# Last keys' scores at an earlier tick in a bank of their own, and part of the sums and statistics of attention on ScalarE, in a Conformer block

## The chip, the cores and the metric

The kernel runs on one core of a Trainium2 chip. The metric is device time in microseconds of one execution. TensorE does the matrix products (PE, with its weight loads as PEld), VectorE (DVE), ScalarE (ACT) and GpSimd (POOL) the rest, and nearly all transfers are started by SyncE's queue (SP).

## The reference

```python
B, T, D, K = (2, 4000, 512, 3);  F = 4 * D
h = _layernorm(x);  h = _silu(h @ w_ff1_a) @ w_ff1_b;  x1 = x + 0.5 * h
h = _layernorm(x1);  q = h @ w_q;  k = h @ w_k;  v = h @ w_v
p = _softmax(jnp.einsum('btd,bsd->bts', q, k) * scale)
x2 = x1 + jnp.einsum('bts,bsd->btd', p, v) @ w_o
h = _layernorm(x2) @ w_pw1
h = h[..., :D] * _sigmoid(h[..., D:])
dc = <three taps along t of h, weights dw>
dc = <normalized per channel over all of B and T>
x3 = x2 + _silu(dc) @ w_pw2
h = _layernorm(x3);  h = _silu(h @ w_ff2_a) @ w_ff2_b;  x4 = x3 + 0.5 * h
return _layernorm(x4)
```

All arrays are bf16.

## The kernel before

**Stages.** The 8000 tokens are cut into 16 chunks (`NCK`), eight for each batch (`TCB`): seven of 512 tokens and a short one of 416. Feed-forward 1 runs over all chunks (0 to 395 us of the profile), then attention over all chunks of queries (395 to 1395), the tail of the convolution (1395 to 1435), and feed-forward 2 (1435 to the end). The layer normalization, projection and first pointwise product of the convolution for chunk `g - 1` run beside the attention of chunk `g`.

**Attention.** A chunk `g` is a loop over 32 ticks `kt`, one for each tile of 128 keys; the last tile has 32 keys. Products are done with seven multiplications in place of eight (on halves). Scores come in quads of four key tiles (`score_quad`, four steps, one for each tick): seven partial products into PSUM banks s0, s1 and s2, with ScalarE copying one bank into another and into SBUF and VectorE adding in between; a later matmul adds onto what VectorE or ScalarE left in the bank. ScalarE's exps write the probabilities. `pair_sums` makes the sums that the products with the values need, and in steps 4 and 5 the row sums of the softmax in an fp32 accumulator `acc`. The products with the values go to banks s3 and y0 to y3.

**The last 32 keys** are handled by `tail_scores`: 16 small matmuls (4 on each of four parts of the array), an exp, a store of the result to DRAM and four loads that spread it over the partitions. It stands at tick 21.

**Beside it** for chunk `g - 1`: at tick 2 `split_sums` splits the row sums into two bf16 parts, two transposing transfers turn them (`sums_by_query`), and VectorE reduces them and takes the reciprocal; at ticks 9 and 13 `project` multiplies two token tiles each by the folded value and output weights, and `residual` adds them, scaled by the reciprocal, to the stream `XT`. Then `ln_job` takes the statistics on VectorE (`bn_stats`, `bn_aggr`), the power -1/2 on GpSimd, the shift on VectorE, the normalization on ScalarE, and a transposing transfer. At ticks 24 and 28, and 3 and 5 of the next chunk, `pw1` uses the result.

**The planner.** The program is written down in this order by ticks, but not issued in it. `Plan` records every operation with the buffers it reads and writes and a duration by a formula (an activation: 170 + 0.83 ns for each element, 200 more where the scale is a per-partition operand), and draws up one order for each engine. TensorE may take matmuls from up to 8 us ahead of the oldest one left. For each other engine the operation with the earliest deadline `late` goes first; `late` is worked back from what waits for it:

```python
n.late = min([s.late - self.lag(n, s) - (self.SPARE if n.size else 0) for s in n.succs] + [pe[min(n.at, len(pe) - 1)].late + 40000])
```

The program also holds a second branch (`any_score`), for inputs with large scores; it does not run here.

In the profile nearly every instruction has line 93, so tiles are named by their memory: `sums` (probabilities and their sums), `keys`, `work` (queries, normalized tokens, row sums, small statistics), `xt` (the residual stream and the streamed key and value sums), `wff` (weights, convolution buffers, `pq` and `ptail` of the last keys), `s` and `y` (the PSUM banks).

Of the kernel before, what the change touches and what calls it, by code (L numbers as in the profile page):

```python
# [15 lines left out]
TILE = 128  # L16
# [93 lines left out]
class Plan:  # L110
# [161 lines left out]
    def once(self):  # L272

        pe, T = self.pe, self.T
        for n in reversed(self.nodes):
            if n.e != "PE":
                n.late = min([s.late - self.lag(n, s) - (self.SPARE if n.size else 0) for s in n.succs] + [pe[min(n.at, len(pe) - 1)].late + 40000])
        free = {e: 0.0 for e in self.AFTER}
# [272 lines left out]
class Conformer:  # L551
# [35 lines left out]
    def memory(self):  # L587
# [503 lines left out]
    def ln_norm(self, c, sl, ti, out, b_out, eng, src=None):  # L1091
# [7 lines left out]
        else:  # L1099
            self.act(out, x, AF.Identity, [b_x, self.b_sh[sl][ti], self.b_rs[sl][ti]], [b_out],  # L1100
                     bias=self.sh[sl][:, ti:ti + 1], scale=self.rs[sl][:, ti:ti + 1])

    def ln_job(self, c, kind, eng="DVE", plan=(1, 1, 2, 2, 3, 4, 5, 5, 6, 6), slot=None, pe=None):

# [120 lines left out]

    def residual(self, ps, b_ps, g, scalar, b_scalar=(), rows=slice(0, TILE)):

        self.S.op("DVE", lambda e: e.scalar_tensor_tensor(
            out=self.XT[g][rows], in0=ps[rows], scalar=scalar, in1=self.XT[g][rows], op0=ALU.mult, op1=ALU.add),
            reads=[b_ps, self.bx[g]] + list(b_scalar), writes=[self.bx[g]])  # L1230

# [524 lines left out]
    def pair_sums(self, g, j, step):  # L1756
# [20 lines left out]
        if step == 6:  # L1777
            S.op("DVE", lambda e: e.tensor_tensor(out=acc[:, 0], in0=acc[:, 0], in1=acc[:, 1], op=ALU.add),
                 reads=[self.b_acc[s]], writes=[self.b_acc[s]])
            return  # L1780
        sig = [ft[:, 0:2, at + k, 0:hw] for k in range(n)]
        if j == 0:
            S.op("DVE", lambda e: e.tensor_copy(acc, sig[0]), reads=b_f[0:2], writes=[self.b_acc[s]])
        elif j == GROUPS - 1:
            S.op("DVE", lambda e: e.tensor_tensor(out=acc, in0=acc, in1=sig[step - 4], op=ALU.add),
                 reads=b_f[0:2] + [self.b_acc[s]], writes=[self.b_acc[s]])
        else:
            two = self.P30[:, 0:W].rearrange("p (h k) -> p h k", h=2)
            out, x, y, rd, b_out = ((two, sig[0], sig[1], b_f[0:2], self.b_P30), (acc, acc, two, [self.b_P30, self.b_acc[s]], self.b_acc[s]))[step - 4]
            S.op("DVE", lambda e: e.tensor_tensor(out=out, in0=x, in1=y, op=ALU.add), reads=rd, writes=[b_out])  # L1790

# [153 lines left out]
    def k_stream(self, g, q):  # L1945
        n, b = (QUADS * g + q) % 2, g // TCB
        self.load(self.KF[n].rearrange("p m u j k -> p (m u j k)"), self.kfd[b][q], self.b_KF[n], reads=[self.b_kfd[b][q]])

# [54 lines left out]

    ASIDE = {3: (5, 7), 4: (5, 7), 5: (5, 7), 6: (5, 7), 16: (0,), 20: (0,), 21: (1,)}
# [148 lines left out]
    def keys_swap(self, g, kt):  # L2153
# [30 lines left out]
    def tail_scores(self, g):  # L2184
# [69 lines left out]
    def sums_by_query(self, s, n=6):  # L2254
# [5 lines left out]
        def reduce():  # L2260
            S.op("DVE", lambda e: e.tensor_reduce(
                self.sq[s], self.sT[0:TILE].rearrange("p h c k -> p c h k"), AX.XY, ALU.add),
                reads=self.b_sT, writes=[self.b_sq[s]])
            S.op("DVE", lambda e: e.reciprocal(self.rl[s], self.sq[s]), reads=[self.b_sq[s]], writes=[self.b_rl[s]])

# [7 lines left out]

    def project(self, g, ti):
        s, r = g % 2, tile_rows(g, ti)
# [7 lines left out]
        self.residual(ps, b_ps, tile_at(g, ti), self.rl[s][r, ti:ti + 1], [self.b_rl[s]], r)  # L2283

# [67 lines left out]
    def pw1(self, t, cb):  # L2352
# [9 lines left out]
        for out, x in moves:  # L2362
            for cc in range(DC):
                self.mm(out, self.Wp1[:, cc, cb * 128:(cb + 1) * 128], x[:, cc], cc == 0, cc == DC - 1,
                        [self.b_Wp1] + self.b_lnT[1 if t == NCK - 1 else 0], b_ps)
        return ps, b_ps
# [207 lines left out]
    def program(self, any_score):  # L2574
# [111 lines left out]
        def att_hook(g, kt):  # L2686
# [285 lines left out]
```

## Time and profile before

| | |
|---|---|
| time, median of 3 runs | 1879.53 us (1877.93 to 1880.09) |
| the profiled execution's own time | 1879.47 us |
| its span in the profile | 1875.6 us |
| granted TensorE clock, mean | 0.998 |
| busy: PE, PEld, DVE, ACT, POOL | 1857.5, 1445.4, 1548.0, 1278.0, 124.2 us |
| feed-forward 1, attention, tail of the convolution, feed-forward 2 | 395, 1000, 40, 441 us |
| one quiet chunk of attention | 62.93 us |

A row of the timeline gives the start of a group of equal instructions, the time to the end of the last, the engine, what it writes and reads, the shapes, the count, and in brackets how long the engine stood idle before it and which engine's result ended that. A row of grouped instructions gives the summed busy time, the mean of one in ns, and the idle time before them.

### The profile page before, as it was taken

How to read it: one execution, taken by the hardware profiler on the slowest of the kernel's cores; microseconds unless marked ns; L12 is line 12 of the kernel's file. 1: busy time of each engine (PE TensorE's matmuls, PEld its weight loads, DVE VectorE, ACT ScalarE, POOL GpSimd, SP SyncE). 2: the span in 40 equal slices, each digit the busy share in tenths (PEclk: the TensorE clock that was granted, in tenths of full speed). 3: DMA queues.
4: the chain of work that ended last, by engine and by line, in shares of the span. 5: the costliest groups of instructions: out<-in, count | busy, mean ns of one | idle time of the engine just before them, and what ended most of it. 6: DMA issues, size and time to landing. Idle time of an engine off the chain costs nothing.

```text
span 1875.6 us, 38994 instructions
## 1 busy us (share of the span) xinstructions
PE 1857.5 (99%) x15384; PEld 1445.4 (77%) x15384; DVE 1548.0 (83%) x3293; ACT 1278.0 (68%) x2190; POOL 124.2 (7%) x241
## 2 busy tenths in 40 slices
PE   9999999999999999999999999999999999999998
PEld 5888888866777777777677777777764888888886
DVE  7789989868778888877878788778878889889885
ACT  5777777754556666666557666666657787777774
POOL 1000000000000000000000001000011000000010
PEclk9999999999999999999999999999999999999999
DMA  7333344197545555448954444444365222221211
GB/s 197 86 89 91 80 112 107 53 275 208 172 142 159 155 171 160 117 130 175 254 123 133 134 119 114 126 138 122 107 205 158 66 69 69 72 54 48 63 33 56
DMA packets 325013, 231.51 MB, mean 123 GB/s; under 512 B 204179, under 2 KB 295638, under 8 KB 324566
## 3 DMA queue, kind: packets, MB, share of 16 engines
q1 hardware_dynamic: 324294, 228.68, 44.2%
q8 instruction: 123, 2.02, 0.4%
q14 instruction: 68, 0.56, 0.1%
q10 hardware_dynamic: 528, 0.26, 0.0%
HBM read 128.44 MB, written 55.79 MB: 98 GB/s over the span
## 4 chain that ended last, share of the span: by engine, by line
PE 97%; DVE 1%; ACT 1%; DMA 0%; issue 0%; SPq 0%; DVEq 0%; ACTq 0%
PE s L93 49%; PE y L93 49%; DVE work L93 1%; ACT work L93 0%; DVE wff L93 0%; DMA xt<-in_x_dram 0%; ACT sums L93 0%; DVE xt L93 0%; DVE s L93 0%; ACT xt L93 0%; ACT s L93 0%; DVE sums L93 0%; DVE keys L93 0%; ACT keys L93 0%; SPq L93 0%
## 5 line engine op out<-in xcount | busy, mean ns | idle before, releaser
L93 ACT ACTIVATE sums<-s 128x512 bf16<-128x512 f32 (+2 forms) x494 | 289.1, 587 | 234.3 <-PE s L93 232.8
L93 ACT ACTIVATE keys<-s 128x512 bf16<-128x512 f32 (+2 forms) x284 | 165.2, 587 | 141.4 <-PE s L93 115.8
L93 DVE TENSOR_TENSOR sums<-sums 128x512 bf16<-128x512 bf16 (+3 forms) x528 | 201.8, 399 | 63.5 <-ACT sums L93 53.1
L93 PE MATMUL y<-work,keys 128*128 128x256 bf16 x1920 | 244.8, 273 | 0.0
L93 PE MATMUL s<-work,keys 128*128 128x256 bf16 (+5 forms) x1456 | 225.1, 292 | 0.8 <-ACT sums L93 0.6
L93 PE MATMUL y<-wff,keys 128*128 128x256 bf16 (+3 forms) x1592 | 209.2, 276 | 0.1
L93 DVE BATCH_NORM_STATS2 work<-xt 128x6 f32<-128x512 bf16 x311 | 205.6, 683 | 3.9 <-DMA xt<-in_x_dram 3.3
L93 PEld LDWEIGHTS y<-work,keys 128*128 128x128 bf16 x1920 | 187.9, 98 | 25.1
L93 PE MATMUL y<-sums,keys 128*128 128x256 bf16 (+1 forms) x1440 | 204.8, 270 | 0.0
L93 PE MATMUL s<-sums 128*128 128x256 bf16 x1296 | 194.5, 273 | 0.0
L93 DVE TENSOR_TENSOR keys<-keys 128x1024 bf16<-128x1024 bf16 (+2 forms) x262 | 170.2, 663 | 26.2 <-ACT keys L93 20.8
L93 PE MATMUL y<-work,wff 128*128 128x256 bf16 (+2 forms) x1116 | 184.0, 292 | 0.0
L93 PEld LDWEIGHTS y<-wff,keys 128*128 128x128 bf16 (+1 forms) x1592 | 151.2, 98 | 32.4 <-issue 3.3
L93 ACT ACTIVATE work<-xt,work 128x512 bf16<-128x512 bf16 x208 | 160.1, 805 | 10.9 <-DVE work L93 9.1
L93 POOL TENSOR_TENSOR work<-work 128x4 f32<-128x4 f32 (+3 forms) x92 | 88.3, 963 | 1108.3 <-DVE work L93 1108.3
L93 PEld LDWEIGHTS y<-sums,keys 128*128 128x128 bf16 x1440 | 139.1, 98 | 22.7 <-issue 0.2
L93 PEld LDWEIGHTS s<-work,keys 128*128 128x128 bf16 (+1 forms) x1456 | 119.3, 97 | 48.2 <-issue 4.7
L93 PEld LDWEIGHTS s<-sums 128*128 128x128 bf16 x1296 | 126.7, 98 | 20.0
L93 PE MATMUL s<-work,wff 128*128 128x512 bf16 (+5 forms) x668 | 140.5, 345 | 1.4 <-ACT work L93 1.1
L93 PE MATMUL y<-sums,xt 128*128 128x256 bf16 (+1 forms) x960 | 141.2, 270 | 0.3 <-DVE sums L93 0.3
L93 PE MATMUL s<-work 128*128 128x512 bf16 (+4 forms) x565 | 137.5, 373 | 2.4 <-DVE work L93 1.7
L93 PEld LDWEIGHTS y<-work,wff 128*128 128x128 bf16 x1116 | 108.2, 98 | 29.7
(140 smaller groups left out, 3195.8 us busy)
## 6 DMA issues: line engine op xcount, KB each, us to landing
xt<-kfd SPq DMA_DIRECT2D x98, 384.0 KB, 3.2
xt<-v12d SPq DMA_DIRECT2D x105, 256.0 KB, 3.0
xd<-xt SPq DMA_DIRECT2D x28, 512.0 KB, 3.0
xt<-xd SPq DMA_DIRECT2D x28, 512.0 KB, 3.8
out_dram<-xt SPq DMA_DIRECT2D x14, 512.0 KB, 2.9
xt<-in_x_dram SPq DMA_DIRECT2D x13, 512.0 KB, 4.1
dcvd<-wff SPq DMA_DIRECT2D x48, 128.0 KB, 2.7
keys<-dcvd SPq DMA_DIRECT2D x12, 512.0 KB, 4.0
```

The source lines that it names most:

```text
L93: return getattr(eng, self.name)(*self.args, **self.kw)
```

## The change

1. `tail_scores` stands at tick 9 in all chunks but the first (there at 21, as before), ahead of the projection, and always takes bank s1.
2. `touch`: where a short chunk's query product leaves the last 96 columns of bank s1 unwritten, one more matmul of 96 columns is done onto them.
3. In `pw1` the second part of a short chunk's product no longer starts with a replacing matmul.
4. Row sums (`pair_sums`): the first group's sums are no longer copied into `acc`; they are added with the first pair's sum. The last group's two sums are first added to each other in bf16, in a new buffer `last7`.
5. Head sums (`sums_by_query`): in place of VectorE's reduce, four ScalarE copies with an accumulator output.
6. Statistics of the normalization ahead of the convolution: `residual` gives the row sum of each token as accumulator output; GpSimd makes the negative mean of it; ScalarE's Square with that as bias gives the sum of squares as accumulator output; GpSimd does the rest (`ln_middle`, `ln_spread`, `ln_rest`, `ln_beside` in place of `ln_job`).
7. The load of the last key tile of the second batch stands 18 ticks earlier.
8. The planner's deadline `late` is at least the time of the operation's own place on TensorE less 8 us.

```diff
-                n.late = min([s.late - ... for s in n.succs] + [pe[min(n.at, len(pe) - 1)].late + 40000])
+                n.late = max(pe[min(n.at, len(pe) - 1)].late - 8000, min([s.late - ... for s in n.succs] + [pe[min(n.at, len(pe) - 1)].late + 40000]))
...
+        self.last7, self.b_last7 = C.view(oLT + 4096, CHUNK), C.buf("last7", oLT + 4096, 2 * CHUNK)
-        self.b_sq = [Buf("sq") for _ in range(2)]
+        self.b_sqs = [[Buf("sq") for _ in range(TPC)] for _ in range(2)]
...
+    def touch(self, ps, b_ps, W):
+        if W < CHUNK and b_ps is self.bank(1)[1]:
+            x = self.hT[0][:, 0, 0, :]
+            self.mm(ps[:, W:CHUNK], x, x[:, 0:CHUNK - W], False, True, [self.b_hT[0][0]], b_ps, skip_group_check=True)
...
+    def ln_middle(self, sl, two):
+        self.S.op("POOL", lambda e: e.tensor_scalar(self.mv[sl][:, two, 0], self.st[sl][:, two, 0], -1.0 / D, None, ALU.mult),
+                  reads=self.b_st[sl][two], writes=self.b_mv[sl][two])
+
+    def ln_spread(self, c, sl, ti):
+        x, b_x = self.tokens(c, ti)
+        self.act(self.ltm[ti][0:TILE, :], x, AF.Square, [b_x, self.b_mv[sl][ti]], [self.b_ltm[ti], self.b_st[sl][ti]],
+                 bias=self.mv[sl][:, ti, 0:1], accum_out=self.st[sl][:, ti, 1:2])
+
+    def ln_rest(self, sl):
+        S = self.S
+        S.op("POOL", lambda e: e.tensor_scalar(self.mv[sl][:, :, 1], self.st[sl][:, :, 1], 1.0 / D, EPS, ALU.mult, ALU.add), ...)
+        S.op("POOL", lambda e: e.tensor_tensor(out=self.rs[sl], in0=self.mv[sl][:, :, 1], in1=self.neghalf[0:TILE], op=ALU.pow), ...)
+        S.op("POOL", lambda e: e.tensor_tensor(out=self.sh[sl], in0=self.mv[sl][:, :, 0], in1=self.rs[sl], op=ALU.mult), ...)
+
+    def ln_beside(self, c, sl, plan):
+        spread, rest, norm = plan[0:4], plan[4], plan[5:9]
+        def tile(ti):
+            self.ln_norm(c, sl, ti, self.ltm[ti][0:TILE, :], self.b_ltm[ti], "ACT")
+            self.transpose(self.lnT[0][:, ti], self.ltm[ti], [self.b_ltm[ti]], [self.b_lnT[0][ti]])
+        for ti in range(TPC):
+            self.after(spread[ti], lambda ti=ti: self.ln_spread(c, sl, ti))
+        self.after(rest, lambda: self.ln_rest(sl))
+        for ti in range(TPC):
+            self.after(norm[ti], lambda ti=ti: tile(ti))
...
     # residual: accum_out=total where a total is given
...
     # q_group, and pw1 where t < NCK - 1
+        self.touch(ps, b_ps, W)
...
     # pair_sums
+        if j == 0:
+            return
         sig = [ft[:, 0:2, at + k, 0:hw] for k in range(n)]
-        if j == 0:
-            S.op("DVE", lambda e: e.tensor_copy(acc, sig[0]), reads=b_f[0:2], writes=[self.b_acc[s]])
-        elif j == GROUPS - 1:
-            S.op("DVE", lambda e: e.tensor_tensor(out=acc, in0=acc, in1=sig[step - 4], op=ALU.add), ...)
+        t, b_t = (self.P30, self.b_P30) if j < GROUPS - 1 else (self.last7, self.b_last7)
+        two = t[:, 0:W].rearrange("p (h k) -> p h k", h=2)
+        if step == 4:
+            out, x, y, rd, wr = two, sig[0], sig[1], b_f[0:2], [b_t]
+        elif j == 1:
+            _, _, f0, b_0 = self.p_home(g, 0)
+            out, x, y, rd, wr = acc, two, f0[:, 0:2, 1, 0:hw], [b_t] + b_0[0:2], [self.b_acc[s]]
+        else:
+            out, x, y, rd, wr = acc, acc, two, [b_t, self.b_acc[s]], [self.b_acc[s]]
+        S.op("DVE", lambda e: e.tensor_tensor(out=out, in0=x, in1=y, op=ALU.add), reads=rd, writes=wr)
...
     # attention, ahead of units_late and units
+                if kt == (9 if g else 21):
+                    self.tail_scores(g)
                 if g:
                     self.units_late(g - 1, kt)
                 self.units(g, kt)
-                if kt == 21:
-                    self.tail_scores(g)
...
     # units_late
+        if kt == 9:
+            self.ln_conv = self.nxt("ln", self.LN_SLOTS)
         for ti in {9: (0, 1), 13: (2, 3)}.get(kt, ()):
-            self.project(o, ti)
+            self.project(o, ti, self.ln_conv)
+            if ti % 2:
+                self.ln_middle(self.ln_conv, slice(ti - 1, ti + 1))
...
     # keys_swap
-                if (6 + k * (2 * KT - 12) // KT if k < KT - 1 else KT + 6) == at:
+                if (6 + k * (2 * KT - 12) // KT if k < KT - 1 else KT - 12) == at:
...
     # tail_scores
-        ps, b_ps = self.sbank()
+        ps, b_ps = self.bank(1)
...
     # sums_by_query, reduce
+            for ti in range(TPC if not self.any_score else 0):
+                x = self.sT[0:TILE, :, ti]
+                self.act(x, x, AF.Copy, self.b_sT, [self.b_sqs[s][ti]], accum_out=self.sq[s][:, ti:ti + 1])
...
     # att_hook
-                self.ln_job(g - 1, "in", "ACT", (1, 2, 5, 6, 7, 8, 8, 9, 10, 11), slot=0)
+                self.ln_beside(g - 1, self.ln_conv, (2, 3, 6, 7, 7, 8, 9, 10, 11))
```

More of the change, by code (lines that the diff above doesn't have):

```diff
@@ L1224, in keys_at, with residual @@
         return self.keysd[b, t0:t0 + n, :], rd + ([self.b_keyst[b]] if t1 >= T - TAIL else [])
-    def residual(self, ps, b_ps, g, scalar, b_scalar=(), rows=slice(0, TILE)):
+    def residual(self, ps, b_ps, g, scalar, b_scalar=(), rows=slice(0, TILE), total=None):
+        more, wr = ({"accum_out": total[0][rows]}, [total[1]]) if total else ({}, [])
         self.S.op("DVE", lambda e: e.scalar_tensor_tensor(
-            out=self.XT[g][rows], in0=ps[rows], scalar=scalar, in1=self.XT[g][rows], op0=ALU.mult, op1=ALU.add),
-            reads=[b_ps, self.bx[g]] + list(b_scalar), writes=[self.bx[g]])
+            out=self.XT[g][rows], in0=ps[rows], scalar=scalar, in1=self.XT[g][rows], op0=ALU.mult, op1=ALU.add, **more),
+            reads=[b_ps, self.bx[g]] + list(b_scalar), writes=[self.bx[g]] + wr)
     def ff_first(self, c, f, p, b_p):
@@ L1946, in k_stream @@
         n, b = (QUADS * g + q) % 2, g // TCB
-        self.load(self.KF[n].rearrange("p m u j k -> p (m u j k)"), self.kfd[b][q], self.b_KF[n], reads=[self.b_kfd[b][q]])
+        self.load(self.KF[n].rearrange("p m u j k -> p (m u j k)"), self.kfd[b][q], self.b_KF[n],
+                  reads=[self.b_kfd[b][q]])
     def score_quad(self, g, q, step):
@@ L2002, in score_quad @@
             exp(h[:, 0:W], b_h, 21)
[L2004 removed]
+    ASIDE = {3: (5, 7), 4: (5, 7), 5: (5, 7), 6: (5, 7), 16: (0,), 20: (0,)}
     def attention(self, old, hook):
@@ L2260, in reduce @@
         def reduce():
[L2261 to L2264, printed above, removed]
+            for ti in range(TPC if not self.any_score else 0):
+                x = self.sT[0:TILE, :, ti]
+                self.act(x, x, AF.Copy, self.b_sT, [self.b_sqs[s][ti]], accum_out=self.sq[s][:, ti:ti + 1])
+            if self.any_score:
+                S.op("DVE", lambda e: e.tensor_reduce(
+                    self.sq[s], self.sT[0:TILE].rearrange("p h c k -> p c h k"), AX.XY, ALU.add),
+                    reads=self.b_sT, writes=self.b_sqs[s])
+            S.op("DVE", lambda e: e.reciprocal(self.rl[s], self.sq[s]), reads=self.b_sqs[s], writes=[self.b_rl[s]])
         self.after(n, reduce)
@@ L2282, in project @@
                     dc == 0, dc == DC - 1, [self.b_Wvo] + [b[dc] for b in parts], b_ps)
-        self.residual(ps, b_ps, tile_at(g, ti), self.rl[s][r, ti:ti + 1], [self.b_rl[s]], r)
+        total = (self.st[sl][:, ti, 0:1], self.b_st[sl][ti]) if sl is not None else None
+        self.residual(ps, b_ps, tile_at(g, ti), self.rl[s][r, ti:ti + 1], [self.b_rl[s]], r, total)
     def sums_direct(self, s):
@@ L2363, in pw1 @@
             for cc in range(DC):
-                self.mm(out, self.Wp1[:, cc, cb * 128:(cb + 1) * 128], x[:, cc], cc == 0, cc == DC - 1,
-                        [self.b_Wp1] + self.b_lnT[1 if t == NCK - 1 else 0], b_ps)
+                self.mm(out, self.Wp1[:, cc, cb * 128:(cb + 1) * 128], x[:, cc], cc == 0 and out is moves[0][0], cc == DC - 1,
+                        [self.b_Wp1] + self.b_lnT[1 if t == NCK - 1 else 0], b_ps, skip_group_check=True)
+        if t < NCK - 1:
+            self.touch(ps, b_ps, W)
         return ps, b_ps
```

15 lines of the change are left out of this document (8 added, 7 removed).

## The prediction

> **What bounds the kernel now.** I read the page first: span, engines, chain.
>
> ```profile
> span 1875.6 us, 38994 instructions
> PE 1857.5 (99%) x15384; PEld 1445.4 (77%) x15384; DVE 1548.0 (83%) x3293; ACT 1278.0 (68%) x2190; POOL 124.2 (7%) x241
> PE 97%; DVE 1%; ACT 1%; DMA 0%; issue 0%; SPq 0%; DVEq 0%; ACTq 0%
> ```
>
> The chain that ended last is 97% TensorE. So an instruction taken off VectorE or put on ScalarE is worth only what it does to TensorE's gaps. Next I asked for busy time by stretch, cut at the stages (feed-forward 1 up to 395 us, attention up to 1395, tail of the convolution up to 1435) and around TensorE's waits, with one quiet chunk of attention as last row.
>
> ```profile
> core 0: us, PE busy (x) PEld busy (x) DVE busy (x) ACT busy (x) POOL busy (x), PEclk, DMA share, GB/s
> 13.00:395.00 382.00, 382.00 (x3344) 325.91 (x3343) 330.01 (x673) 287.26 (x485) 29.45 (x29) 1.00 0.41 105
> 395.00:500.00 105.00, 104.79 (x729) 68.31 (x727) 82.04 (x209) 52.85 (x89) 4.03 (x4) 1.00 0.73 216
> 500.00:864.00 364.00, 363.49 (x3005) 276.30 (x3004) 297.59 (x653) 235.98 (x413) 17.55 (x49) 1.00 0.54 151
> 864.00:895.00 31.00, 30.32 (x281) 22.83 (x279) 22.03 (x53) 23.01 (x45) 2.11 (x5) 1.00 0.71 162
> 895.00:950.00 55.00, 54.14 (x364) 32.32 (x362) 42.16 (x103) 27.84 (x48) 2.29 (x8) 1.00 0.88 228
> 950.00:1355.00 405.00, 405.00 (x3352) 307.84 (x3350) 327.92 (x699) 268.87 (x470) 21.67 (x71) 1.00 0.45 124
> 1355.00:1395.00 40.00, 38.05 (x393) 31.94 (x392) 30.32 (x71) 24.68 (x48) 2.03 (x5) 1.00 0.57 182
> 1395.00:1435.00 40.00, 34.77 (x188) 16.76 (x187) 33.20 (x75) 24.88 (x46) 8.43 (x23) 0.96 0.67 207
> 627.52:690.45 62.93, 62.93 (x515) 47.66 (x514) 52.82 (x117) 42.16 (x75) 3.60 (x9) 1.00 0.59 167
> ```
>
> The order of the built program differs between the two kernels only in attention: in feed-forward 1, in the tail of the convolution and in feed-forward 2 every engine's instructions stand as they stood. In attention TensorE is idle 0.21 + 0.51 + 0.68 + 0.86 + 0 + 1.95 = 4.2 us. The 5.2 us idle of 1395 to 1435 lie behind the last difference.
>
> A quiet chunk has no idle time in 62.93 us, with VectorE at 52.8 and ScalarE at 42.2. So what can be won is in a few places. The timeline shows what one looks like:
>
> ```profile
> 498.22 0.61 PE L93 MATMUL s<-xt 128*128 128x256 bf16 x4
> 498.67 0.60 PE L93 MATMUL s<-work,keys 128*128 128x256 bf16 x4
> 498.94 0.70 DVE L93 TENSOR_TENSOR s<-s,xt 128x512 f32<-128x512 f32 x1 [0.24 <-ACT work L93]
> 499.10 0.38 PE L93 MATMUL y<-sums,xt 128*128 128x256 bf16 x2
> 499.69 0.61 PE L93 MATMUL s<-xt,keys 128*128 128x256 bf16 x4 [0.21 <-DVE s L93]
> ...
> 504.77 0.61 PE L93 MATMUL s<-xt 128*128 128x256 bf16 x4
> 505.21 0.60 PE L93 MATMUL s<-work,keys 128*128 128x256 bf16 x4
> 505.48 0.70 DVE L93 TENSOR_TENSOR s<-s,xt 128x512 f32<-128x512 f32 x1 [0.75 <-PE s L93]
> ...
> 506.24 0.61 PE L93 MATMUL s<-xt,keys 128*128 128x256 bf16 x4 [0.43 <-DVE s L93]
> ```
>
> Four matmuls of 256 columns start 0.44 us apart, 0.109 each. A score quad's loop (product, VectorE's sum, next product) takes 499.69 - 498.22 = 1.47 us from start to start. At 498.22 the order holds 4 + 4 + 2 matmuls in it, 1.09 us: short by 0.38. At 504.77 it holds 8, 0.87 us: short by 0.60. A last matmul's record runs 0.16 beyond its pace (0.60 for four, of which 0.44 is pace), so the idle column shows 0.21 and 0.43. **These gaps are loops with too few matmuls in them, not a full VectorE**: it was idle 0.24 and 0.75 us before those two sums. With the 0.16 added back at some 17 gaps, attention loses 4.2 + 2.7 = 6.9 us: the most that any relief can return.
>
> **The change, part by part.** The prices:
>
> ```profile
> L93 DVE BATCH_NORM_STATS2 work<-xt 128x6 f32<-128x512 bf16 x311 | 205.6, 683 | 3.9 <-DMA xt<-in_x_dram 3.3
> L93 DVE BATCH_NORM_AGGREGATE work<-work 128x2 f32<-128x9 f32 x315 | 48.0, 180 | 2.1
> L93 DVE SCALAR_TENSOR_TENSOR work<-work 128x4 f32<-128x4 f32 x71 | 11.5, 162 | 8.4 <-POOL work L93 7.8 <-DVE sums L93 0.3
> L93 DVE TENSOR_REDUCE work<-work 128x4 f32<-128x1024 bf16 x14 | 17.0, 1215 | 2.2 <-DMA work<-work 2.2
> L93 DVE CAST work<-sums 128x512 f32<-128x512 bf16 x14 | 5.9, 418 | 0.0
> L93 DVE TENSOR_TENSOR work<-work,sums 128x512 f32<-128x512 f32 x28 | 19.2, 684 | 0.1
> L93 ACT ACTIVATE sums<-s 128x512 bf16<-128x512 f32 x336 | 199.7, 596 | 206.8 <-PE s L93 205.5
> L93 ACT ACTIVATE wff<-wff,work 128x512 bf16<-128x512 bf16 x146 | 101.4, 713 | 0.0
> L93 ACT ACTIVATE wff<-s 128x128 bf16<-128x128 f32 x14 | 4.0, 283 | 0.0
> L93 ACT ACTIVATION_READ_ACCUMULATOR work<-s 128x1 f32 x4 | 0.8, 194 | 0.0
> L93 ACT ACT_TABLE_LOAD x5 | 6.4, 1283 | 2.9 <-PE s L93 1.6 <-PEq L2957 1.2
> L93 POOL TENSOR_TENSOR work<-work 128x4 f32<-128x4 f32 x73 | 76.4, 1047 | 1027.0 <-DVE work L93 1027.0
> L93 POOL TENSOR_SCALAR wff<-work 128x1 f32<-128x1 f32 x4 | 1.3, 317 | 0.3
> ```
>
> *VectorE* loses per chunk four statistics (2.73 us), four aggregates (0.72), the shift (0.16), the reduce over the head sums (1.22), the cast that began the row sum (0.42), and one of the last group's two fp32 adds becomes a bf16 add (0.684 - 0.42 = 0.27): 5.5 us of 52.8. It gains an accumulator output on four residuals. No row shows VectorE reading one; nearest is ScalarE's read, 0.19, so 0 to 0.8 us a chunk, and I take 0.4. None of this is on the path in a quiet chunk: worth 0 there.
>
> The Trainium skill (VectorE: DVE Perf Modes, Two Vector instructions with no wait between them) says that an operation with an accumulator output is two instructions; no run shown here has one on VectorE. By that rule the four reads do stand in its queue, and they would still be covered by the 5.5 us removed.
>
> *ScalarE* gains per chunk four Squares over 512 columns with one per-partition operand. Between 0.60 (no such operand) and 0.71 (one) plus a read of 0.19; the 0.71 row fits, and neighbours overlap by about 0.1, so 0.8 us each, 3.2. Four copies of 256 elements: between 0.28 (128) and 0.60 (512), 0.39 on the line, with the read about 0.5 each, 2.0. 42.2 becomes 47.4 us of 62.9. Covered as long as no exp waits too long behind them (second rival).
>
> *GpSimd* gets two small scalings before the Squares and, behind them, one scaling and one more multiply: 3 x 0.32 + 1.05 = 2.0 us on 3.6. The normalization starts later by the chain scaling, Square, scaling, power, multiply, but its ticks are unchanged and the first pointwise product comes seven ticks behind it (seven times 62.93 / 32 = 13.8 us). Covered.
>
> *Last keys' scores.* 16 small matmuls, an exp of 0.28, a store and four loads on SP's queue go from tick 21 to tick 9 of a chunk, past 12 ticks of the streams of key and value sums. On TensorE they cost the same anywhere. Behind the moved exp, in bank 1, a projection must wait; the order keeps six to eight matmuls there, at least 0.65 us, against 0.16 for the product's end, 0.28 for the exp and two handovers of 0.05 to 0.1: 0 to 0.05 us a chunk, and with a longer handover 0.3 in all, which I take. The four loads wait for the store while the next key sums' load stands behind them; those are loaded about five ticks (9.8 us) ahead. 0, or if that cover is short, one load's delay of under 1 us in a chunk.
>
> *The touches.* The built program has four extra matmuls of 96 columns (the bank matters only for two of four query groups in each of the two short chunks): 0.04 us each by the pace, at most 0.15 with an unhidden weight load: 0.2 to 0.6, I take 0.2.
>
> *Order.* Attention's order is drawn anew, since costs and the deadline floor (8 us before an operation's own place) changed. So I applied the same arithmetic as at 498.22 to every place of both orders where a product waits for one ScalarE or VectorE instruction: matmuls between at their pace, against row durations. Shortages over 0.1 us:
>
> - old order: 0.37, 0.15, 0.59 (the first score quads, 499 to 506 us); 0.39, 0.57, 0.14 (first short chunk); 0.28, 0.71 (start of the second batch); 0.32, 0.57, 0.50, 0.55, 0.57, 0.14 (last chunk). Sum 5.9, where the trace loses 6.9.
> - new order: 0.37, 0.15, 0.50; a new 0.50 in the chunk before the short one; 0.39, 0.21, 0.57, 0.14; 0.50; a new 0.50 before the last chunk; 0.14, 0.57, 0.85, 0.50, 0.39. Sum 6.3.
>
> The 0.60 at 505 us goes, because the new order puts 14 matmuls there; two of 0.50 come in. Net +0.4 us, uncertain by about 1.
>
> **Sum**, against the profiled execution's own 1879.47 us (0.06 below the median 1879.53 of the runs): +0.4 (loops) + 0.2 (touches) + 0.3 (bank 1), of which about half may overlap other gaps, gives about **1880.0 us**; own range 1878.5 to 1881.5.
>
> **Rivals.**
>
> *Relief.* With VectorE 5.5 us lighter per chunk, its sums come at once and most gaps close. For it: TensorE's waits in attention name VectorE's results in most places. Against it: VectorE idled before the sums at 498.94 and 505.48, and the new order still holds loops that are too short whatever VectorE does. Two thirds of 6.9 us gone: 1875. Chance 0.13.
>
> *ScalarE's queue becomes the bound.* It works in order, and exps that free score banks stand behind the Squares. What such a bunch does is in the trace:
>
> ```profile
> 1368.04 2.92 ACT L93 ACTIVATE work<-xt,work 128x512 bf16<-128x512 bf16 x4
> 1370.86 0.50 ACT L93 ACTIVATE sums<-s 128x416 bf16<-128x416 f32 x1
> 1372.35 0.52 PE L93 MATMUL s<-xt 128*128 128x208 bf16 x4 [0.57 <-ACT sums L93]
> ```
>
> In a quiet chunk of the new order two Squares stand between a copy and an exp; from the end of that exp's product to the next writer of its bank are 14 matmuls, 1.53 us. Less 0.16 for the product's end, 0.60 for the exp and two handovers of 0.05 to 0.1, it may start 0.6 late. Its product ends about 1.2 us behind the copy; two Squares at 0.8 take 1.6, so it starts 0.4 late. It decides from about 0.9 us a Square, or if the scaling on GpSimd comes over 0.2 us late, for a Square that waits holds the exp too. The planner's own cost of an activation counts neither the per-partition bias nor the read, so it did not leave room for them on purpose. At 1.1 us: 0.4 us in each of 15 chunks, 6 us: 1885.5. Chance 0.17.
>
> *Table switches.* If Square were missing beside exp, up to 60 Squares would bring two loads each, 154 us on ScalarE and, in front of exps, at least a third of that on TensorE: 1930. The Trainium skill (ScalarE: Activation LUTs, Table sets: the hidden batching unit) says that functions come in sets and that changing sets costs a load. The built program has five table loads, as before, at the same stages: this is out, below 0.01.
>
> That the work isn't moved at all is out too: the built order has 164 instructions fewer on VectorE.
>
> **How the numbers follow.** Forecast 0.69, relief 0.13, ScalarE's queue 0.17, the rest 0.01. 0.2% is 3.8 us, about what a measurement of this kernel can tell (three runs spread over 2.2 us). The forecast lies wholly within it, most of relief below 1875.8, most of the queue case above 1883.3: faster 0.13, same 0.69, slower 0.18. The range reaches to the nearer part of both rivals: 1876.0 to 1884.0.
>
> **What would show it.** Right: quiet chunks still take 62.9 us each with no idle on TensorE, VectorE near 48 and ScalarE near 47 us in them; gaps of some 0.5 us just before the two short chunks; no gap of 0.4 at 505 us; the tail of the convolution as before. Wrong: quiet chunks longer than 62.93 us with waits for ScalarE's exps (second rival), or TensorE's waits in attention under 2 us in sum (relief).

## The result, and the profile after

The changed kernel takes 1887.18 us (median of five runs, 1885.75 to 1889.21) against 1879.53 for the kernel before in runs beside it: ratio 1.0041, 95% interval 1.0026 to 1.0056. It is slower by some 7.6 us; the forecast was 1880.0 with a range up to 1884.0. The profiled execution took 1887.44 us.

The page of the changed kernel: span, engines, and the shares of the chain that ended last.

```profile
span 1883.5 us, 39160 instructions
...
PE 1861.0 (99%) x15388; PEld 1441.9 (77%) x15388; DVE 1485.6 (79%) x3189; ACT 1336.3 (71%) x2421; POOL 141.1 (7%) x301
...
PE 93%; ACT 3%; DVE 2%; DMA 1%; issue 0%; SPq 0%; POOL 0%; DVEq 0%; ACTq 0%
```

VectorE went from 83% to 79%, ScalarE from 68% to 71%: the work was moved as meant. But the chain, 97% TensorE before, is now 93% TensorE, and ScalarE has 3% of it, DMA 1%. Busy time by stretch, cut as before, with one quiet chunk as the last row:

```profile
core 0: us, PE busy (x) PEld busy (x) DVE busy (x) ACT busy (x) POOL busy (x), PEclk, DMA share, GB/s
13.00:395.00 382.00, 382.00 (x3346) 325.98 (x3344) 330.52 (x675) 287.46 (x485) 29.50 (x29) 1.00 0.42 105
...
500.00:864.00 364.00, 361.88 (x2977) 272.26 (x2978) 271.93 (x609) 256.39 (x500) 23.51 (x70) 1.00 0.53 149
864.00:895.00 31.00, 28.25 (x250) 21.53 (x248) 18.37 (x46) 22.66 (x47) 3.02 (x8) 1.00 0.87 166
...
950.00:1355.00 405.00, 403.63 (x3326) 303.72 (x3324) 297.80 (x645) 291.64 (x564) 28.52 (x98) 1.00 0.44 125
...
629.00:691.94 62.94, 62.50 (x511) 46.81 (x509) 48.30 (x110) 45.41 (x89) 4.26 (x13) 1.00 0.58 165
```

TensorE was idle 0.5 us from 500 to 864 and never from 950 to 1355 us; now it is 2.1 and 1.4. In the first short chunk (864 to 895) its idle time rose from 0.7 to 2.8 us. The granted clock is 1.00 in all of these. TensorE's waits name what is new:

```profile
PE s L93 <- ACT s L93: 2.9, 4, 0.9
PE y L93 <- DMA xt<-v12d: 1.9, 2, 1.7
...
PE s L93 <- ACT sums L93: 1.4, 3, 0.7
...
PE s L93 <- DVE s L93: 0.8, 3, 0.4
```

The first two groups were not in the list of before. VectorE's sums (the last row) stood there with 1.4 us:

```profile
PE s L93 <- DVE s L93: 1.4, 4, 0.4
```

That they fell to 0.8 is not shown to be relief of VectorE. Of the 0.6 us, 0.43 is the gap at 506.24 us, which was forecast to go because the new order holds more matmuls there. The other 0.18 is a gap in the last chunk (0.41 at 1382 us before, 0.23 at 1390 us now), whose shortage was forecast to fall from 0.57 to 0.39.

**A tally of stalls.** From each trace I took the time from one matmul's start to the next less the pace of its shape, wherever this was over 0.1 us, and added it up over attention (490 to 1400 us). It contains the 0.16 us that the idle column leaves out. Places whose record is missing are left out too. One profile per kernel, so differences under about 1 us are not read.

| us | quiet chunks | before the short chunks (819, 1322) | first short chunk | rest | attention |
|---|---|---|---|---|---|
| before | 0.0 | 0.0 | 1.4 | 5.5 | 6.9 |
| changed | 1.7 | 2.0 | 3.9 | 6.1 | 13.7 |

The difference of 6.8 is nearly all of the loss of 7.6. Where the rest of it lies, the first and last of one group of attention's matmuls show, before and changed:

```profile
L93 PE MATMUL y<-sums,keys x1440: 252/273/284, 418.3 to 1390.2; 128*128 128x256 bf16 x158, 128*128 128x208 bf16 x22
L93 PE MATMUL y<-sums,keys x1440: 252/272/283, 418.2 to 1397.7; 128*128 128x256 bf16 x158, 128*128 128x208 bf16 x22
```

From 418 us to the last of them attention takes 971.9 us before and 979.5 in the changed kernel, 7.6 longer; from there to the end of the span it is 485.4 and 485.8. So the loss lies in attention, and the tally misses some 0.8 us of it; three places are to be explained. Below, this stretch is called attention's length; two profiles of the same program (the changed kernel and run 10) differ by 1.1 us in it.

### The profile page after: what moved, and what is told of

It reads as the page before. It is cut to its first block, busy times and chain, and to the rows that moved or that the text cites. A ratio compares the mean times of both kernels' runs of the same rounds, so it can differ in the third digit from the quotient of the medians.

```text
span 1883.5 us, 39160 instructions
## 1 busy us (share of the span) xinstructions
PE 1861.0 (99%) x15388; PEld 1441.9 (77%) x15388; DVE 1485.6 (79%) x3189; ACT 1336.3 (71%) x2421; POOL 141.1 (7%) x301
## 4 chain that ended last, share of the span: by engine, by line
PE 93%; ACT 3%; DVE 2%; DMA 1%; issue 0%; SPq 0%; POOL 0%; DVEq 0%; ACTq 0%
PE s L93 47%; PE y L93 46%; ACT work L93 1%; DVE work L93 1%; DMA work<-work 1%; ACT sums L93 1%; ACT xt L93 0%; ACT keys L93 0%; DVE keys L93 0%; DVE wff L93 0%; SPq L93 0%; DVE xt L93 0%; DVE s L93 0%; ACT s L93 0%; DVE sums L93 0%
## 5 line engine op out<-in xcount | busy, mean ns | idle before, releaser
L93 ACT ACTIVATE work<-xt,work 128x512 bf16<-128x512 bf16 x268 | 202.7, 785 | 10.2 <-DVE work L93 8.5
L93 DVE BATCH_NORM_STATS2 work<-xt 128x6 f32<-128x512 bf16 x251 | 165.9, 682 | 4.5 <-DMA xt<-in_x_dram 3.8
```

Of the source, the lines that this page charges most:

```text
L93: return getattr(eng, self.name)(*self.args, **self.kw)
```

## The experiments

Times are medians beside runs of the kernel before, which gave 1879.58 to 1880.18; ratios carry a 95% interval. "Order held" means that the planner draws the order for the changed kernel's instructions, and only when an instruction is emitted is another put in its place. So nothing else moves. The "one-hop arithmetic" is the forecast's: the matmuls between two products at their pace, against the one ScalarE or VectorE instruction that the second product waits for.

**1. Head sums on VectorE, order held** (`sums_by_query`: of the four planned copies three emit nothing, the fourth emits the reduction).

```
 self.act(x, x, AF.Copy, ..., accum_out=self.sq[s][:, ti:ti + 1])
+S.plan.nodes[-1].emit = [] if ti < TPC - 1 else [lambda: S.emit_op("DVE", <tensor_reduce over sT>)]
```

> The changed kernel with every engine's order held as it is, but in place of the four ScalarE copies that sum the head sums, one VectorE reduction as in the kernel before, put where the last copy stood. Theory 1 (ScalarE's in-order queue waits for the transposing transfer in front of these copies and holds copies and exps behind it): the idle 16 us in front of them leaves ScalarE, the quiet chunks' extra stalls of TensorE (some 1.6 us in sum) go or halve, total 1885.5 to 1886.3. Theory 2 (only the redrawn order costs, wherever the sums are computed): every stall stays, 1887.2. Theory 3 (any queue that waits there stalls TensorE): VectorE now waits some 16 us in that place and the stalls stay or grow, 1887 to 1889.

Measured: 1885.10 us, 1.0028 (1.0017 to 1.0038). Stalls of the quiet chunks 1.7 to 0.5; 819 and 1322 stay at 2.0. In time the gain is not clear of the noise: the interval overlaps that of the changed kernel, and attention's length, 978.4 us, is that of run 10, its repeat. Why the stalls went, the group rows of the head sums show, first the changed kernel:

```profile
L93 ACT ACTIVATE work<-work 128x256 bf16<-128x256 bf16 x56 | 22.8, 409 | 16.2 <-DMA work<-work 16.1
```

then this run:

```profile
L2312 DVE TENSOR_REDUCE work<-work 128x4 f32<-128x1024 bf16 x14 | 17.0, 1213 | 0.4 <-DMA work<-work 0.4
```

ScalarE stood idle 16.1 us in all, 1.15 us a chunk, in front of the first copy, waiting for the transposing transfer `work<-work`. VectorE had stood 2.2 us there in the kernel before, and at the last copy's place in the new order it stands 0.4. In the timeline of the changed kernel one sees what queues behind that wait:

```profile
651.66 2.50 SPq L93 DMA_TRANSPOSE work<-work  x2
...
656.88 0.42 ACT L93 ACTIVATE work<-work 128x256 bf16<-128x256 bf16 x1 [2.52 <-DMA work<-work]
...
657.21 0.19 ACT L93 ACTIVATION_READ_ACCUMULATOR work<-work 128x1 f32 x1
657.30 0.58 ACT L93 ACTIVATE sums<-s 128x512 bf16<-128x512 f32 x1
...
659.65 0.42 ACT L93 ACTIVATE work<-work 128x256 bf16<-128x256 bf16 x1
...
660.05 0.41 ACT L93 ACTIVATE work<-work 128x256 bf16<-128x256 bf16 x1
...
660.59 0.18 DVE L93 RECIPROCAL work<-work 128x4 f32<-128x4 f32 x1 [0.17 <-ACT work L93]
...
662.15 0.60 ACT L93 ACTIVATE xt<-s 128x512 f32<-128x512 f32 x1
...
662.78 0.58 ACT L93 ACTIVATE s<-s 128x512 f32<-128x512 f32 x1
...
663.41 0.61 PE L93 MATMUL s<-xt 128*128 128x256 bf16 x4 [0.44 <-ACT s L93]
```

After 2.52 us of waiting, exps, copies and the four accumulations follow without a gap until 662.78; the score quad's second copy (`s<-s`) comes late, and TensorE waits.

**2. Statistics on VectorE too, order held** (statistics, aggregates and shift emitted where Squares and scalings stood).

```
 self.act(..., AF.Square, ...)              # ln_spread
+self.S.plan.nodes[-1].emit = [<bn_stats of x on DVE>]
 S.op("POOL", <1 / D and EPS>)              # ln_rest; its last multiply likewise becomes the shift on DVE
+S.plan.nodes[-1].emit = [<bn_aggr on DVE> for ti in range(TPC)]
```

> The same order held, head sums on VectorE, and in place of the Squares VectorE's statistics (four statistics, four aggregates, the shift), put where the Squares and scalings stood; the row sums on the residuals stay and are overwritten. Theory 'Squares hold the exps': the quiet chunks lose further stalls against the run before it, 0.5 to 1.5 us. Theory 'order': stalls at 819, 878 and 1322 us stay as they are, total within 1 us of the run before it. If VectorE's fullness is what the change relieves, VectorE at 84% brings stalls of 1 us and more in the quiet chunks instead.

Measured: 1903.69 us, 1.0132 (1.0117 to 1.0148): 18.6 us slower than run 1, stalls in every chunk. In its timeline a statistic now stands in front of a score sum:

```profile
685.14 0.68 DVE L1118 BATCH_NORM_STATS2 work<-xt 128x6 f32<-128x512 bf16 x1
685.74 0.68 DVE L93 TENSOR_TENSOR s<-s,xt 128x512 f32<-128x512 f32 x1
...
686.48 0.61 PE L93 MATMUL s<-xt,keys 128*128 128x256 bf16 x4 [0.82 <-DVE s L93]
```

This order leaves VectorE no place there. It does not say that the statistics are dear in an order drawn for them:

**8. Statistics back on VectorE, order drawn anew.**

```
-self.project(o, ti, self.ln_conv)          # and no ln_middle
+self.project(o, ti)
-self.ln_beside(g - 1, self.ln_conv, (2, 3, 6, 7, 7, 8, 9, 10, 11))
+self.ln_job(g - 1, "in", "ACT", (1, 2, 5, 6, 7, 8, 8, 9, 10, 11), slot=0)
```

> The changed kernel with the statistics of the convolution's normalization back on VectorE and the order drawn anew for that. With the order held this cost 18.6 us; if that was because the order had left VectorE no place, the redrawn order brings it back to the changed kernel's time within 2 us (1886 to 1889). If VectorE lacks the time itself, 1895 or more. If Squares on ScalarE delay exps, this is faster than the changed kernel, 1885 or less.

Measured: 1887.51 us, 1.0043 (1.0030 to 1.0057), level with the changed kernel. Taking the Squares back gains nothing, so the theory that they hold exps finds no support. The order is another one here, with a stall of its own (1.0 us at 569); what clears the Squares is run 9 below, which has them and is level with the kernel before.

**3. The last keys' transposing load 18 ticks later, as before** (`keys_swap`). Only the DMA queue's order differs.

```
-else KT - 12) == at
+else KT + 6) == at
```

> The changed kernel with the transposing load of the second batch's last keys put back 18 ticks, where it was before. Only the DMA queue's order differs; every compute engine's order is the same instruction for instruction. Theory 'the load order delays a value-sum load': the stall of 1.84 us at 878 us goes, the first short chunk (875 to 890) loses about 2 us and not 3.9, total 1885.4. Rival (the delay comes from the key-sum loads and transposes ahead of it, or from the last keys' stores and loads): the stall stays or moves to the next load, 1887.2. The other stalls stay under both.

Measured: 1884.12 us, 1.0026 (1.0017 to 1.0035), 3.1 below the changed kernel; first short chunk 3.9 to 1.8. The DMA queue and TensorE's wait in the changed kernel:

```profile
866.46 1.19 SPq L93 DMA_TRANSPOSE keys<-tailsd  x1
...
875.49 0.43 SPq L93 DMA_DIRECT2D xt<-v12d  x1
875.97 1.63 SPq L93 DMA_TRANSPOSE keys<-keysd  x1
877.64 5.27 SPq L93 DMA_TRANSPOSE work<-work  x4
...
880.44 0.35 PE L93 MATMUL y<-sums,xt 128*128 128x208 bf16 x2 [1.68 <-DMA xt<-v12d]
...
884.38 1.89 PE L93 MATMUL s<-work,wff 128*128 128x512 bf16 x8 [0.34 <-DMA work<-work]
```

and in this run:

```profile
875.34 0.59 SPq L93 DMA_DIRECT2D xt<-v12d  x1
875.97 5.19 SPq L93 DMA_TRANSPOSE work<-work  x4
...
879.21 0.35 PE L93 MATMUL y<-sums,xt 128*128 128x208 bf16 x2 [0.16 <-DMA xt<-v12d]
```

One transposing load less in that stretch, and the four transposes of the normalized tokens are issued 1.7 us earlier, and the pointwise product `s<-work,wff` no longer waits. Which transfer is late varies: run 10 below is the same program as the changed kernel and had no stall at 879 us but one of 1.3 us at 883, in front of that product. The chunk's sum does not hang on that: 2.9 to 4.1 with the early load (the changed kernel, runs 1, 8, 10, 11, 14; in runs 2 and 12 the chunk's bounds moved too far for the tally), 1.4 to 2.0 without it (the kernel before, runs 3 to 7, 9, 13, 15, 16).

**4. The reverse of run 1: the kernel before, order held, head sums by four ScalarE copies** at the reduction's place.

```
 S.op("DVE", <tensor_reduce over sT>, ...)
+S.plan.nodes[-1].emit = [<ACT copy of sT[:, :, ti], accum_out sq[:, ti]> for ti in range(TPC)]
```

> The kernel before with every engine's order held, but the head sums' reduction done by four ScalarE copies with an accumulator output in place of one VectorE reduction, at its place in the order. Theory 1 (ScalarE's queue in front of the transposing transfer): ScalarE idles several us in all in front of these copies, quiet chunks that had no stall get some of 0.1 to 0.6 us, total 1880.5 to 1882. Theory 2 (order alone): no new stalls beyond 0.3 us, 1879.5.

Measured: 1883.44 us, 1.0019 (1.0010 to 1.0028). Nine new stalls of 0.26 to 0.58 us in quiet chunks, 3.9 in sum. ScalarE's wait in front of the copies is only 3.0 us in all here, so the copies' own time does it:

```profile
595.48 0.41 ACT L2265 ACTIVATE work<-work 128x256 bf16<-128x256 bf16 x1
...
597.09 0.42 ACT L2265 ACTIVATE work<-work 128x256 bf16<-128x256 bf16 x1
...
599.82 0.58 ACT L93 ACTIVATE s<-s 128x512 f32<-128x512 f32 x1
...
600.46 0.61 PE L93 MATMUL s<-xt 128*128 128x256 bf16 x4 [0.36 <-ACT s L93]
```

Three copies from 595.48 to 597.09 are 0.54 us each; four, 2.2 us, that nothing made room for hit the same place, the second copy of a score quad. The waits stand elsewhere: four over 0.1 us, at 471, 529, 908 and 1094 us, and the first four stalls (600 to 790 us) have none in front of them. This run makes the copies dearer than they are in the changed kernel, though: here all four name one buffer as their output, and each starts only after the accumulator read of the one before (597.09 behind a read that starts at 596.87 and takes 0.19). In the changed kernel, with a buffer for each, they stand 0.40 us apart (659.65 and 660.05 above).

**5 and 6. The tail scores' part taken out, and with it the head sums** (order drawn anew; in 6 also `sums_by_query` as before).

```
-if kt == (9 if g else 21): self.tail_scores(g)       # ahead of units_late
+if kt == 21: self.tail_scores(g)                     # behind units
-ps, b_ps = self.bank(1)                              # tail_scores; ASIDE with 21: (1,) again
+ps, b_ps = self.sbank()
-else KT - 12) == at                                  # keys_swap; no touches, start flags as before
+else KT + 6) == at
```

> The changed kernel without the part on the last keys' scores: scores, touches, the start flags in the pointwise projection and the early load of the last keys as in the kernel before; row sums, head sums, Squares and the deadline floor stay. The order is drawn anew. Theory: this part's redrawn order makes the two stalls of 1.02 us before the short chunks (819, 1322 us) and, by its load, the 1.84 us at 878; all three go, the quiet chunks' stalls from the head sums (some 1.6 us) stay: 1887.2 - 2.0 - 2.4 = 1882.8. Rival (the stalls before the short chunks come with the work moved to ScalarE, which puts an exp between two copies): they stay, about 1885.

> Only Squares, row sums and deadline floor of the change; tail scores and head sums as in the kernel before, order drawn anew. Theory (the loss is the tail scores' order and load plus the head sums in ScalarE's queue, nothing else): as the kernel before, within 1 us: 1878.5 to 1880.5, quiet chunks without stalls. Theory 'Squares hold the exps': quiet chunks keep stalls, 1881 or more. Relief of VectorE: 1876 or less.

Measured: 1885.06 us, 1.0026 (1.0016 to 1.0035), and 1882.88, 1.0014 (1.0005 to 1.0024). In both the stalls at 819 and 1322 are gone and the first short chunk has 1.8. But the quiet chunks have 4.9 and 2.2: the wait for the head sums' transfer came up elsewhere. The executions of these two runs spread wide, 1881.5 to 1889.5 us and 1880.2 to 1887.4 (the other versions over at most 5.2), and the profiled ones took 1887.96 and 1884.32, so the tallies lie above what the medians had. In run 6 it is VectorE that waits:

```profile
843.68 1.22 DVE L93 TENSOR_REDUCE work<-work 128x4 f32<-128x1024 bf16 x1 [1.91 <-DMA work<-work]
...
846.07 0.58 DVE L93 TENSOR_TENSOR xt<-s,xt 128x416 f32<-128x416 f32 x1
...
846.71 0.53 PE L93 MATMUL s<-xt,keys 128*128 128x208 bf16 x4 [1.01 <-DVE xt L93]
```

So it is not ScalarE as such: in either queue the planner may put the head sums before the transfer lands. The engine's idle time in front of them is 16.1 us on ScalarE in the changed kernel and 6.2 in run 5, 5.6 on VectorE in run 6, 2.2 in the kernel before. The planner's landing (`Plan.once`) makes 0.4 + 131072 / 180 ns + 1.0 = 2.1 us from issue for one such transfer with the pipe empty. The query on that tile's two transfers at 651.7 us in the changed kernel answers

```profile
DMA to landing us min/median/max: 2.4/3.2/3.9
```

**7. Both mended, order held** (runs 1 and 3 together).

> The changed kernel with its compute order held, head sums by one VectorE reduction at the last copy's place, and the last keys' load put back 18 ticks. If both effects are separate they add up: 1887.2 - 2.1 - 3.1 = 1882.0, with the stalls at 819 and 1322 us (1.02 each) still there, none at 878 above 0.4 and none above 0.3 in the quiet chunks. If the load's delay only moves from chunk to chunk, 1884 to 1885.

Measured: 1884.16 us, 1.0022 (1.0013 to 1.0031); tally 10.7, where 13.7 less the savings of runs 1 and 3 (0.8 and 1.8) is 11.1: in stalls they add up. In time they do not: it is level with run 3 and 2.2 us above what was expected. Attention's length says where: 978.4, 977.5 and 976.2 us in runs 1, 3 and 7, that is 1.1, 2.0 and 3.3 below the changed kernel's, so there they do add up. But the stretch behind attention, where runs 3 and 7 have one order, took 484.1 us in the one profile and 485.8 in the other.

**10 and 11. Later head sums, and a later landing in the planner** (all parts kept).

```
-self.sums_by_query(o % TCB % 2, 5)             # run 10
+self.sums_by_query(o % TCB % 2, 6)
-n.land = pipe - s + 1000                        # run 11 (runs 9, 14, 16 too; 15 with 3000)
+n.land = pipe - s + (2500 if n.turn else 1000)
```

> The changed kernel with the head sums' copies allowed one tick (1.97 us) later. Theory: ScalarE's idle time in front of them falls from 16 us to under 6, the quiet chunks' stalls fall from 1.6 to under 0.5 us, the stalls at 819, 878 and 1322 us stay: 1885.5 to 1886. Rival: the projections' residuals, which need the reciprocal about 1 us behind the last copy, come late and bring as much: 1887 or more.

> The changed kernel, all parts, with the planner's landing of transposing transfers 1.5 us later. Theory: quiet chunks' stalls under 0.5 us, and the planner, knowing later transfers, may place the value-sum loads otherwise so that the stall at 878 us changes; 819 and 1322 us stay: 1884 to 1886. Rival: the order is drawn worse elsewhere, 1887 or more.

Measured: run 10 gave 1886.38 us, 1.0034 (1.0021 to 1.0048), but it tests nothing: the planner drew the same order, instruction for instruction, so it is a repeat of the changed kernel, with 16.9 us of ScalarE's wait and a tally of 12.7. Run 11: 1886.01 us, 1.0031 (1.0019 to 1.0042); the copies stay on ScalarE and the wait is gone,

```profile
L93 ACT ACTIVATE work<-work 128x256 bf16<-128x256 bf16 x56 | 22.6, 417 | 0.5 <-DMA work<-work 0.4
```

and the quiet chunks have 0.4. What remains is 2.0 at 819 and 1322 and 4.1 in the short chunk.

**9. Later landing, without the tail scores' part.**

> The changed kernel without the part on the last keys' scores, and with the planner told that a transposing transfer lands 1.5 us later than it assumed (2500 ns behind its place in the pipe in place of 1000). Theory (head sums stand too early in an in-order queue because their transfers land later than planned; the tail scores' order costs the rest): the stalls at 845 and 1287 us and in the quiet chunks go, no 1.02 us at 819 and 1322; stalls of attention 490 to 1400 us in sum near the one-hop arithmetic's 4.0 + 17 x 0.1 = 5.7 to 7 us, against 6.9 of the kernel before: 1878 to 1880. Rival (the transfers' lateness varies and no fixed landing covers it): 1882 to 1885 as without the landing.

Measured: 1879.62 us, 0.9997 (0.9988 to 1.0006): level with the kernel before, with Squares and head sums on ScalarE and the shorter row sums. VectorE's relief and ScalarE's load are then together worth nothing that can be measured, and the whole loss of the change goes with the tail scores' part and the landing. One wait of 0.81 us is left in a quiet chunk, at 644 us, behind VectorE's wait of 1.46 for another load (`wff<-keysd`). The two causes do not add up: on its own the landing returned 1.2 us (run 11) and leaving out the tail scores' part 2.1 (run 5), both together 7.6.

**12 and 14. The tail scores' part alone on the kernel before, and the same with the later landing.**

> The kernel before with the last keys' part alone (scores earlier and in bank 1, touches, start flags, early load); no sums move to another engine. One-hop arithmetic on its order (matmuls between, at their pace, against one ScalarE or VectorE instruction) gives shortages of 9.5 us where the kernel before has 5.0, the new ones at 625, 687, 857 to 875, 1058, 1121 and 1247 us: 1884 if the part costs by the order it draws. If it costs by the load of the last keys only: 1881 to 1882. If it cost nothing by itself: 1879.5.

> The kernel before with the last keys' part alone, and the planner's landing of transposing transfers 1.5 us later. Without the landing this part cost 14 us, with VectorE's head-sum reduction waiting for its transfer in front of the score sums. Theory (the wait for the late transfer is most of it): stalls in quiet chunks fall from 9 to under 3 us, the two 1.02 us before the short chunks appear as in the changed kernel: 1884 to 1888. Theory (VectorE is too full for this part without the Squares' relief): quiet stalls stay over 6 us, 1890 or more.

Measured: 1893.92 us, 1.0076 (1.0062 to 1.0089), and 1886.71, 1.0036 (1.0022 to 1.0050). Alone it costs 14.0 us, nearly twice what the whole change does and 10 us more than the one-hop arithmetic gave; VectorE waits 11.6 us in front of its reductions, and the quiet chunks have 9.6. With the landing mended 7.2 us come back, and the pair at 819 and 1322 appears. So lateness was about half of it, as far as a redrawn order can say, and VectorE was not too full.

**13. Three exps put behind the second copy, otherwise as run 7.**

```
 self.act(m5, h, AF.Copy); ...              # as drawn: copy, exp of another quad, copy
-exp; self.act(h, c, AF.Copy)
+self.act(h, c, AF.Copy); exp
```

> The run with head sums on VectorE and the last keys' load put back, every order held but for three pairs on ScalarE: in each an exp that stands between the two copies of a first score quad (at 819, 1322 and 1379 us) is put behind the second copy. Theory (the stall is the 0.50 us of the one-hop arithmetic plus about 0.5 us of an exp standing in front of the copy): the stalls of 1.02 us fall to 0.45 to 0.6 each, the one of 0.86 near 1378 us by 0.3 to 0.5: 1884.2 - 1.3 = 1882.9. Rival (the exp frees a bank that TensorE needs as soon as the copy): the stalls move a few matmuls on and the sum stays.

Measured: 1885.24 us, 1.0028 (1.0019 to 1.0038); the rival held, and more: at each of the first two places the stall of 1.02 became two, 0.65 and 1.00 us, so the exp's bank was needed next, and the sum there grew. In the changed kernel it reads

```profile
818.39 0.60 PE L93 MATMUL s<-work,keys 128*128 128x256 bf16 x4
...
818.65 0.60 ACT L93 ACTIVATE xt<-s 128x512 f32<-128x512 f32 x1 [0.43 <-PE s L93]
818.83 0.60 PE L93 MATMUL y<-sums,keys 128*128 128x256 bf16 x4
...
819.15 0.59 ACT L93 ACTIVATE sums<-s 128x512 bf16<-128x512 f32 x1
819.62 0.60 ACT L93 ACTIVATE s<-s 128x512 f32<-128x512 f32 x1
...
820.28 0.61 PE L93 MATMUL s<-xt 128*128 128x256 bf16 x4 [0.85 <-ACT s L93]
```

Copy, exp and copy follow each other at 0.5 us without a gap, while TensorE has the 8 matmuls from 818.39 to cover them: three instructions of ScalarE are the loop, in whatever order. A copy on VectorE might be the cure; that was not tried.

**15 and 16. Towards a faster version**: run 9 with a landing of 3000, and the kernel before with the landing of 2500 alone (the one line shown for run 11).

> The changed kernel without the last keys' part, landing of transposing transfers 2 us later (the run with 1.5 us later was level with the kernel before). One-hop arithmetic gives shortages of 3.7 us where that run had 4.0 and the kernel before 5.0: 1878 to 1879.5, a gain of at most 1 us, if no transfer is late; level at 1880 otherwise.

> The kernel before, with nothing but the planner's landing of transposing transfers 1.5 us later. VectorE's wait in front of the head sums (2.2 us in 14) goes; the one-hop arithmetic gives the same shortages as before (5.0), so TensorE gains nothing: 1879 to 1880. If late transfers cost the kernel before something that its stalls do not show, 1878 or less.

Measured: 1879.43 us, 0.9997 (0.9988 to 1.0006), and 1879.57, 1.0000 (0.9991 to 1.0009). No version beat the kernel before; its attention is 971.9 us long, and the shortest of all the others, run 16, has 971.8.

## Why the prediction was wrong

- **What bounds it, and relief**: right. VectorE lost 4 points of its share, and TensorE's waits for its sums fell by 0.6 us, at places where the new order was forecast to be less short of matmuls; run 9 shows that the moved work is together worth nothing.
- **Prices of the moved instructions**: near, and on the safe side. Two Squares take 1.41 us from start to start, 0.71 each for a forecast 0.8:

```profile
672.74 0.71 ACT L93 ACTIVATE work<-xt,work 128x512 bf16<-128x512 bf16 x1
...
673.44 0.71 ACT L93 ACTIVATE work<-xt,work 128x512 bf16<-128x512 bf16 x1
...
674.15 0.58 ACT L93 ACTIVATE sums<-s 128x512 bf16<-128x512 f32 x1
```

  A copy takes 0.40 in the changed kernel (0.54 in run 4) for a forecast 0.5. In the quiet chunk shown above ScalarE's busy time rose by 3.3 us (42.16 to 45.41) and not by 5.2; what makes up the difference is open. On VectorE the accumulator's read is a row of its own, which the Trainium skill (VectorE: DVE Perf Modes, Two Vector instructions with no wait between them) led to expect; the trace agrees:

```profile
L93 DVE DVE_READ_ACCUMULATOR xt<-s,work,xt 128x1 f32 x59 | 4.9, 83 | 0.0
```

  Four of them are 0.33 us a chunk where I took 0.4.
- **The failed step, "Covered as long as no exp waits too long behind them"** (head sums on ScalarE): I priced the copies by their busy time, and put the second rival's danger on the Squares. The row of the reduction that they replace said `2.2 <-DMA work<-work 2.2`, that is, its input sometimes lands late. I quoted it and did not ask what queues behind that wait once it is ScalarE's. It measured 16.1 us of ScalarE's idle time and, by runs 1 and 11, 1.2 to 1.3 us of stalls in quiet chunks. In time that is 1.2 to 2.1 us (0.4 to 1.3 against run 10, the repeat), which lies within the noise. The second rival had the right engine and the wrong instructions.
- **The failed step, "0, or if that cover is short, one load's delay of under 1 us in a chunk"** (DMA queue): I counted the tail scores' store and loads, but not the transposing load of the last keys that the same part moves 18 ticks ahead, and I called the normalized tokens' transposes covered by seven ticks. Run 3 gives 2.3 to 3.1 us (against run 10 and the changed kernel); the stalls that went are in the short chunk, 3.9 to 1.8.
- **The mis-sized term, two new loops of "0.50"**: right places, 1.02 each. The arithmetic took one ScalarE instruction between two products; three stand there. That is +1.0 us more than forecast. Elsewhere the arithmetic held: no such stalls in the orders where it gave none (5, 6, 9, 15). In the first score quads it missed one of 0.51 at 503 us, part of the rest's 0.6.
- **Bank 1 and the touches**, 0.3 and 0.2: no stall shows at the projection behind the moved exp; they weren't measured alone.

So the sum's +0.4 for the order was too small, and two terms that it put at 0 were not. What stays open: what else in the tail scores' part costs (from run 11 to run 9 it is 6.4 us, of which the early load is 2.3 to 3.1 and the two loops 2.0), and why the landing and this part cost together more than the sum of what each returns alone.

## What to carry to other kernels

Before a reduction moves to another engine, read what its input waits for: an instruction that waits for a transfer holds everything behind it in an in-order queue, and the price is the wait plus the backlog (here 2.52 us of waiting at 656.88, and no gap until 662.78), not its busy time. When an order is drawn by a planner, compare its assumed landings with the profile's; here 1.5 us decided more than all the moved work, and any edit redraws the places where it shows. To tell a moved instruction's cost from that of the redrawn order, hold the order and exchange only what is emitted.

## What the runs showed of the hardware

Two executions of one program let the same load land 4.9 and at most 3.4 us after its issue (`xt<-v12d` at 875.5 and 875.2 us, changed kernel and run 10), and TensorE's stall moved with it from 878 to 883 us. An accumulator's read takes 83 ns on VectorE and 190 on ScalarE.
